# Two kept products ahead of the fourth chunk, and an imaginary weight of mode 0 that is not read, in a fused attention and spectral-mixing kernel

## The chip, the cores and the metric

The kernel runs on one core of a Trainium2 chip. The metric is device time in microseconds of one execution. A core has a matrix engine (PE, with PEld for its weight loads), a vector engine (DVE), a scalar engine (ACT), GpSimd (POOL), which here issues the loads, SyncE (SP), which here issues the small copies and the stores, and 16 DMA engines that all transfers share.

## The reference

Attention with a learned decay runs first; its output is the input of a spectral layer: a Fourier transform along the sequence (576 positions), the 64 lowest modes each multiplied by a complex 512x512 matrix, the inverse transform, and a last matrix with a ReLU.

```python
def _moe_ref(x, w_r, w_i, w_ch):          # x: 8 x 576 x 512, the attention's output
    X = np.fft.rfft(x, axis=1)
    Xr, Xi = (np.real(X[:, :n_modes]), np.imag(X[:, :n_modes]))
    Yr = np.einsum('bmd,mde->bme', Xr, w_r) - np.einsum('bmd,mde->bme', Xi, w_i)
    Yi = np.einsum('bmd,mde->bme', Xr, w_i) + np.einsum('bmd,mde->bme', Xi, w_r)
    Y[:, :n_modes] = Yr + 1j * Yi
    y = np.fft.irfft(Y, n=S, axis=1)
    u = x + y
    return u + np.maximum(u @ w_ch, 0.0)
```

For mode 0 the imaginary part Xi is a sum of x times sin(0), so it is zero, and the inverse transform multiplies Yi of mode 0 by sin(0). The matrix `w_i` of mode 0 therefore has no part in the output.

## The kernel before

**Attention and transform.** The 512 channels are cut into NG = 4 groups of 128 (two heads each), and the attention runs over N = 32 steps n, one for each group and batch. A step makes scores, exponentials and the products with v, then `fft` writes the group's 64 modes into `xs`. The loads of q, k, v for the steps ahead and of the weights `w_r`, `w_i` are issued by POOL in one order (`load`, L220); they are read as fp32 and written as bf16.

**The weights.** A tile holds 4 modes of one group and one of the two weights (ri = 0 real, 1 imaginary): `wq` (L182) lists them as (g, c, ri, par), where c is one of 8 chunks of 8 modes and par its half. There are 128 tiles, 32 for each group. A tile is loaded by two transfers (L210 to L216): even modes into partitions 0 to 63, odd ones into 64 to 127, two modes and 256 KB of bf16 each. The first 8 tiles lie in memory that is free at the start; later ones in rings of buffers, for the last group in one ring of 11 (`wpool`). A tile's load waits until the products of the tile 11 places before it are done.

**The modes.** `modes(g, c)` (L442) makes 16 products of 512 columns that fill one PSUM bank `yp`, four side by side in the columns of the array (128 rows by 32 columns each); x = 0, 1 are those with the real weight, x = 2, 3 with the imaginary one. The results of the groups are added in `y_acc`. In the last group the sum is `y_sb`, in fp16.

**The last group.** After the attention (L573) POOL issues all loads that are left. Per chunk c, L773 to L795 go: `modes`, then `y_transposed` (4 transpositions of `y_sb`, one copy by ACT), and from c = 4 on `y_times_wch` (4 products with `w_ch`). After c = 3 `gather` brings the first four chunks into the order that the inverse transform needs (`yv`); after c = 5 it does so for chunks 4 and 5.

**Kept products.** The output comes in 18 pairs of 128-row blocks. x times `w_ch` doesn't depend on the weights of the modes, so for 16 pairs it is made early and kept in SBUF. 10 of them (`late`, L701) are made in the last group: a call of `work` (L689) transposes the x of one pair (`x_transposed`, L604) and makes the product of the pair before it (`keep`, L625; ACT copies it, and for half of the pairs DVE subtracts). `TAKE` (L703) says how many calls each chunk has; `gather` after c = 3 has two more (turns 1 and 3). `places` (L592 to L595) are 9 places for kept products, the tenth takes a ring buffer. Pairs 0 and 1 are not kept: their products (`x_times_wch`, L616) stay in PSUM for the end.

**The end.** The modes of c = 7 are made with other work in between: `first_u` ahead of x = 2, `first_z` ahead of x = 3 (L798 to L808). Then PE makes the inverse transforms of all pairs, ACT and DVE finish them, and SP stores them.

Of the kernel before, what the change touches and what calls it, by code (L numbers as in the profile page):

```python
# [18 lines left out]
def kernel(  # L19
# [15 lines left out]
    P = 128  # L35
# [10 lines left out]
    MC = 8  # L46
    NCK = NM // MC
# [10 lines left out]
    HP = P // 2  # L58
# [87 lines left out]
    def loads_qkv(n):  # L146

        if n >= N:
            return []
        g, b = divmod(n, B)  # L150
        hs = slice(2 * g, 2 * g + 2)
        q2 = qkpool.tile([P, R + 1, D], BF16, name="q2", tag="q2")[:, :R, :]
        k2 = qkpool.tile([P, R + 1, D], BF16, name="k2", tag="k2")[:, :R, :]
        loaded[n] = (q2, k2)
        todo = [
            (dst, src[b, hs].rearrange("h (p r) d -> (h p) r d", r=R))
            for src, dst in ((q, q2), (k, k2))
        ]
        todo += [
            (  # L160
                v2[n % NV][:, : 2 * NWN * W].rearrange("p (w h c) -> p w h c", w=NWN, h=2)[:, :, h, P:],
                v[b, 2 * g + h, : NF * P, :].rearrange("(w p r) d -> p w (r d)", p=P, r=2),
            )
            for h in range(2)
        ]
        return todo

    def loads_tails(g):

        if g >= NG:  # L170
            return []
        return [
            (
                v4[g % 2][NL * h : NL * h + NL, :, :D],
                v[:, 2 * g + h, NF * P :, :].rearrange("b t d -> t b d"),
            )
            for h in range(2)
        ]
# [11 lines left out]
    wt = {}  # L190
# [3 lines left out]
    def ring_of(k):  # L194
        if k < NE:
            return None
        return int(k < LW2 and (k - NE) % (WA + WB) >= WA)

    def loads_w(upto):
        todo = []  # L200
        while len(wt) < min(upto, len(wq)):
            g, c, ri, par = key = wq[len(wt)]
            i = ring_of(len(wt))
            if i is None:
                t = early[len(wt)]
            else:
                t = (wpool, wpool2)[i].tile([P, WM, DM], BF16, name="w_sb", tag="w")
            src = (moe_w_r, moe_w_i)[ri]
            m0 = c * MC + par * MC // 2
            for h in range(2):  # L210
                todo.append((
                    t[HP * h : HP * h + HP].rearrange("p (m q) e -> p m (q e)", q=2),
                    src[m0 + h : m0 + MC // 2 : 2, g * P : (g + 1) * P, :].rearrange(
                        "m (p q) e -> p m (q e)", q=2
                    ),
                ))  # L216
            wt[key] = t
        return todo
# [34 lines left out]
    first, second, tails0 = loads_qkv(0), loads_qkv(1), loads_tails(0)  # L253
    load(first[:2])
    load(loads_w(W0), first[2:] + tails0 + second)
    nc.sync.dma_start(out=Ff_sb, in_=d_Ff.rearrange("(T p) c -> p T c", p=P))
    nc.sync.dma_start(out=ident16h, in_=d_ident16h)
# [184 lines left out]
    def modes(g, c, meanwhile=None):  # L442


        ps = auxpool.tile([P, DM], FP32, name="yp", tag="aux")
        cols = xs[g % 2].rearrange("p q k h r b m -> p q k (h r b) m")

        def product(ri, q_, cg):
            nc.tensor.matmul(  # L449
                ps[32 * cg : 32 * cg + 32, :],  # L450
                cols[:, q_, 1 - ri, :, c * MC // 2 + cg],
                wt[(g, c, ri, cg // 2)][:, 2 * (cg % 2) + q_, :],
                start=(ri == 0 and q_ == 0), stop=(ri == 1 and q_ == 1),
                tile_position=(0, 32 * cg), skip_group_check=True,
            )

        for x in range(4):
            ri, y = divmod(x, 2)
            if meanwhile and x in meanwhile:
                meanwhile[x]()  # L460
            for z in range(4):
                if meanwhile:
                    product(ri, z // 2, 2 * y + z % 2)
                else:
                    product(ri, y, z)
        if g == 0:
            nc.vector.tensor_copy(out=y_acc[:, c, :], in_=ps)
        elif g < NG - 1:
            nc.vector.tensor_tensor(out=y_acc[:, c, :], in0=ps, in1=y_acc[:, c, :], op=ALU.add)
        else:  # L470
            yb = spool.tile([P, DM], FP16, name="y_sb", tag="y")
            for cols in halves if c == NCK - 1 else [slice(0, DM)]:
                nc.vector.tensor_tensor(
                    out=yb[:, cols], in0=ps[:, cols], in1=y_acc[:, c, cols], op=ALU.add
                )
            if c >= NCK - 2:
                spread(c, 0, yb)
            return yb
# [3 lines left out]
    def spread(c, which, rows):  # L482

        nc.sync.dma_start(out=yv[16 * c : 16 * c + 16, :, which, :], in_=rows)
# [97 lines left out]
    upool = ctx.enter_context(tc.tile_pool(name="u_psum", bufs=2, space=PSUM))  # L582
    zpool = ctx.enter_context(tc.tile_pool(name="z_psum", bufs=2, space=PSUM))

    NLOC = 4
    old = xs_flat[0]
    xt_sb = [
        old[:, i * 2 * DM : (i + 1) * 2 * DM].bitcast(FP16).rearrange("p (x t c) -> p x t c", x=2, c=P)
# [3 lines left out]
    places = [finpool.tile([P, 4 * DM], BF16, name="r_sb", tag="r", bufs=3) for i in range(2)]  # L592
    places += [finpool.tile([P, 4 * DM], BF16, name=f"z1_{i}") for i in range(NLOC)]
    places.append(old[:, 4 * DM : 8 * DM])
# [3 lines left out]
    def parts(b, T):  # L598

        if T < NF:  # L600
            return [(slice(0, P), b, ident16h)]
        return [(slice(NL * i, NL * i + NL), b + i, ident16h[:NL, :NL]) for i in range(2)]

    def x_transposed(i):  # L604
        xts[i] = xt_sb[len(xts) % 2]
        for x, (b, T) in enumerate(pairs[i]):
            ps = upool.tile([P, DT, P], FP32, name="xt_ps", tag="u")
            for rows, bb, ident in parts(b, T):
                for dt in range(DT):
                    nc.tensor.matmul(  # L610
                        ps[:, dt, rows], x_all[: rows.stop - rows.start, dt, bb, T, :],
                        ident, start=True, stop=True, skip_group_check=True,
                    )
            nc.vector.tensor_copy(out=xts[i][:, x], in_=ps)

    def x_times_wch(i, last):  # L616
        zs[i] = z = zpool.tile([P, 2, DM], FP32, name="z_ps", tag="z")
        for x in range(2):
            for dt in range(DT):
                nc.tensor.matmul(  # L620
                    z[:, x, :], xts[i][:, x, dt, :], wch_sb[:, dt, :],
                    start=(dt == 0), stop=(last and dt == DT - 1), skip_group_check=True,
                )
# [13 lines left out]
    NY = NCK // 2  # L637
    yt_first = finpool.tile([P, DT, NY, P], FP16, name="yt_first")

    def y_transposed(yb, c=NCK):  # L640
        ps = auxpool.tile([P, DT, P], FP16, name="yt_ps", tag="aux")
        for dt in range(DT):
            nc.tensor.transpose(ps[:, dt, :], yb[:, bass.ts(dt, P)], ident16h)
        yt = yt_first[:, :, c % NY, :] if c < NCK - 2 else spool.tile([P, DT, P], FP16, name="yt_sb", tag="yt")
        nc.scalar.copy(out=yt, in_=ps)
        return yt

    def y_times_wch(c, yt):
        vp = auxpool.tile([P, DM], FP32, name="v_ps", tag="aux")
        for dt in range(DT):  # L650
            nc.tensor.matmul(
                vp, yt[:, dt, :], wch_sb[:, dt, :], start=(dt == 0), stop=(dt == DT - 1)
            )
        vb = spool.tile([P, DM], FP16, name="v_sb", tag="v")
        nc.vector.tensor_copy(out=vb, in_=vp)
        spread(c, 1, vb)
        return vb
# [31 lines left out]
    def work():  # L689

        if not order_z and not ahead:
            return
        if order_z:
            i = order_z.pop(0)
            x_transposed(i)
            ahead.append(i)
        if len(ahead) == 2 or not order_z:
            i = ahead.pop(0)
            keep(i)

    late = [i for i in kept if i not in first_pairs]  # L701
    order_z = list(late)
    TAKE = (3, 2, 2, 0, 1, 1)  # L703
    us, rs = {}, {}
    GK = P - 2 * MC * NX

# [66 lines left out]
    for c in range(NCK - 2):  # L773
        yb = modes(NG - 1, c)
        for x in range(TAKE[c] - 1):
            work()
        if c == NCK - 3:
            x_transposed(0)
        yt = y_transposed(yb, c)
        if TAKE[c]:  # L780
            work()
        if c >= NY:
            y_times_wch(c, yt)
            if c == NCK - 3:
                gather(NY, NCK - 2, (), (0,))
        elif c == NY - 1:
            gather(0, NY, (1, 3), (1, 0))
    assert not order_z and not ahead
    c = NCK - 2
    x_times_wch(0, False)  # L790
    yb6 = modes(NG - 1, c)
    x_transposed(1)
    yt = y_transposed(yb6)
    x_times_wch(1, False)
    vb6 = y_times_wch(c, yt)  # L795


# [104 lines left out]
```

## Time and profile before

| | |
|---|---|
| median of 11 runs | 454.19 us (452.46 to 455.35) |
| the profiled execution | 453.26 us, its span 451.5 us |
| PE busy | 356.1 us (79%) |
| DVE, ACT, POOL busy | 257.4, 222.0, 241.1 us |
| moved by DMA | 93.83 MB, mean 208 GB/s |
| weight transfers by POOL | 120 + 120 in `w_sb`, 256 KB each, 8.0 and 8.1 us to landing; 16 more into other tiles |
| products of `modes` (L449) | 480 in the records, 444 ns each |

Times of the profile run from the first instruction of the span. Each digit of a row of slices is the busy share of one fortieth of the span. In a row of the timeline come start and duration in us, the engine, the line, the operation, the tiles, how many were merged, and in brackets the engine's idle time before it with what ended it.

### The profile page before, as it was taken

The page shows a single profiled execution, that of the slowest core. Times are in us where ns is not written, and L with a number is a line of the kernel's source. Part 1 is how long each engine was busy: PE and PEld are TensorE (multiplying, and loading weights), DVE is VectorE, ACT ScalarE, POOL GpSimd, SP SyncE. Part 2 cuts the span into 40 slices and gives each one's busy share as a digit, 9 for nine tenths or more (in the row PEclk, how much of TensorE's full clock was granted, in tenths as well). Part 3 has the DMA queues.
Part 4 walks back from the last instruction along what each step waited for, and adds up shares of the span by engine and source line. Part 5 has one row for each costly group of instructions (what it writes and reads, how often), then busy time and mean ns, then how long its engine had stood idle before and what let it go on. Part 6 is the DMA issues. An engine that isn't in the chain of part 4 may idle for free.

```text
span 451.5 us, 11547 instructions
## 1 busy us (share of the span) xinstructions
PE 356.1 (79%) x4713; PEld 225.4 (50%) x4745; DVE 257.4 (57%) x599; ACT 222.0 (49%) x390; POOL 241.1 (53%) x397
## 2 busy tenths in 40 slices
PE   1789988998574979856978687778897778879995
PEld 1466666565443656633546454556564335534432
DVE  7675767574333646733436545546656443662796
ACT  1585778366232745743426443556551223331774
POOL 7766665755566666555665765565544444420000
PEclk9996999897567969987659968989999986999999
DMA  9999999999999999999999999999999999994688
GB/s 180 201 204 206 204 204 205 205 206 207 208 207 202 200 186 200 208 208 206 204 203 207 207 206 207 207 205 201 205 210 211 209 209 209 210 219 91 234 300 316
DMA packets 77797, 93.83 MB, mean 208 GB/s; under 512 B 30433, under 2 KB 40161, under 8 KB 77745
## 3 DMA queue, kind: packets, MB, share of 16 engines
q0 software_dynamic: 68240, 81.81, 104.8%
q1 hardware_dynamic: 9504, 11.29, 7.9%
q8 instruction: 37, 0.61, 0.5%
q14 instruction: 16, 0.12, 0.1%
HBM read 164.56 MB, written 9.44 MB: 385 GB/s over the span
## 4 chain that ended last, share of the span: by engine, by line
DMA 48%; PE 33%; DVE 10%; issue 4%; POOL 2%; ACT 1%; DVEq 0%; POOLq 0%; ACTq 0%
DMA w_sb<-in_moe_w_i_dram 26%; DMA w_sb<-in_moe_w_r_dram 7%; DMA q<-in_q_dram 7%; PE av_ps L401 4%; PE yp L449 4%; PE sc_ps L372 4%; PE ft_ps L427 3%; DMA k<-in_k_dram 3%; PE sc_ps L366 3%; PE tr_ps L331 2%; DVE qtB L334 2%; PE z_ps L620 2%; PE z_ps L711 2%; DVE qtA L334 2%; PE g_ps L670 2%
## 5 line engine op out<-in xcount | busy, mean ns | idle before, releaser
L380 ACT ACTIVATE p_sb<-sc_ps,cumt_sb 128x576 f16<-128x576 f32 (+1 forms) x256 | 141.8, 635 | 59.0 <-PE sc_ps L372 58.6
L224 POOL DMA_DIRECT2D w_sb<-in_moe_w_r_dram x120 | 71.6, 597 | 60.3 <-DMA w_sb<-in_moe_w_r_dram 18.5
L224 POOL DMA_DIRECT2D w_sb<-in_moe_w_i_dram x120 | 71.5, 596 | 49.3 <-DMA w_sb<-in_moe_w_i_dram 15.8
L224 POOL DMA_DIRECT2D v<-in_v_dram x72 | 51.8, 719 | 25.3 <-DMA w_sb<-in_moe_w_i_dram 7.6
L366 PE MATMUL sc_ps<-negm,ident 128*128 128x256 bf16 x256 | 56.8, 309 | 0.2
L449 PE MATMUL yp<-w_sb,xs 128*32 128x512 bf16 x480 | 39.9, 444 | 10.0 <-DMA w_sb<-in_moe_w_i_dram 5.6
L401 PE MATMUL av_ps<-v,p_sb 128*128 128x65 f16 x1024 | 46.1, 201 | 0.0
L334 DVE COPY ktA<-tr_ps 64x576 bf16<-64x576 bf16 x32 | 24.0, 749 | 36.1 <-PE tr_ps L331 36.1
L331 PE MATMUL tr_ps<-ident,q 64*64 64x64 bf16 x576 | 17.2, 209 | 34.1 <-DMA q<-in_q_dram 34.0
L401 PEld LDWEIGHTS <-p_sb 128*128 128x128 f16 x1024 | 40.2, 102 | 5.3 <-DVE x_all L411 2.0
L334 DVE COPY qtA<-tr_ps 64x576 bf16<-64x576 bf16 x32 | 23.8, 743 | 30.7 <-PE tr_ps L331 30.6
L372 PE MATMUL sc_ps<-qtA,ktA 65*128 65x512 bf16 (+2 forms) x192 | 38.3, 311 | 0.6 <-DMA qtA<-ncum_sb 0.6
L351 ACT ACTIVATE p<-sc_ps,cumt 128x64 f16<-128x64 f32 x32 | 10.0, 313 | 55.5 <-PE sc_ps L347 55.5
L437 DVE CAST xs<-ft_ps 64x128 bf16<-64x128 f32 x128 | 31.4, 284 | 9.1 <-PE ft_ps L427 8.7
L372 PE MATMUL sc_ps<-qtB,ktB 128*128 128x64 bf16 (+2 forms) x160 | 33.7, 314 | 3.3 <-issue 2.0
L406 DVE TENSOR_REDUCE den<-av_ps 128x5 f32<-128x10 f32 x64 | 10.8, 169 | 44.3 <-PE av_ps L401 43.5
L427 PE MATMUL ft_ps<-Ff_sb,x_all 128*64 128x96 f16 (+1 forms) x640 | 34.0, 228 | 1.0 <-DVE x_all L411 1.0
L331 PE MATMUL tr_ps<-ident,k 64*64 64x64 bf16 x576 | 16.7, 205 | 20.4 <-DVE qtB L334 10.8
L411 DVE TENSOR_TENSOR x_all<-av_ps,rcp 128x320 f16<-128x320 f32 x64 | 31.5, 492 | 2.2
L334 ACT COPY ktB<-tr_ps 64x576 bf16<-64x576 bf16 x32 | 20.3, 633 | 24.5 <-DVE ktA L334 23.4
L331 PEld LDWEIGHTS <-q 64*64 64x64 bf16 x576 | 13.4, 121 | 36.7 <-DMA q<-in_q_dram 35.5
L449 PEld LDWEIGHTS <-xs 128*32 128x32 bf16 x512 | 19.3, 147 | 24.1 <-issue 13.5
(117 smaller groups left out, 555.7 us busy)
## 6 DMA issues: line engine op xcount, KB each, us to landing
w_sb<-in_moe_w_r_dram POOLq DMA_DIRECT2D x120, 256.0 KB, 8.0
w_sb<-in_moe_w_i_dram POOLq DMA_DIRECT2D x120, 256.0 KB, 8.1
q<-in_q_dram POOLq DMA_DIRECT2D x32, 144.0 KB, 7.3
k<-in_k_dram POOLq DMA_DIRECT2D x32, 144.0 KB, 7.2
v<-in_v_dram POOLq DMA_DIRECT2D x72, 64.0 KB, 7.0
out_dram<-r_sb SPq DMA_DIRECT2D x16, 256.0 KB, 2.2
out_dram<-r_w SPq DMA_DIRECT2D x16, 256.0 KB, 2.7
x_all<-in_moe_w_i_dram POOLq DMA_DIRECT2D x6, 256.0 KB, 7.2
```

The costliest lines, as they stand in the source:

```text
L224: nc.gpsimd.dma_start(out=dst, in_=src)
L331: nc.tensor.transpose(ps[rows, r, :], src[rows, r, :], ident16[rows, rows])
L334: copy(out=dst[n % NQ][rows, :].rearrange("d (p r) -> d p r", r=R), in_=ps[rows].rearrange("d r p -> d p r"),)
L366: nc.tensor.matmul(ps[:, bass.ds(w * S, W)], ident16, negm[:, bass.ts(r, W)], start=True, stop=False, skip_group_check=True,)
L372: nc.tensor.matmul(ps[:, c0 : c0 + i1 - i0], keys[:, w, r, :], qt[:, i0:i1], start=False, stop=True, skip_group_check=True,)
L380: nc.scalar.activation(out=pt[:, poff[x] : poff[x] + S - w * W], in_=ps[:, w * S : (w + 1) * S - w * W], func=ACTF.Exp, bias=cumt_sb[:, x, ...
L401: nc.tensor.matmul(ps[:, I, r : r + NCH], lhsT, rhs, start=(i == 0), stop=(i == len(todo) - 1), skip_group_check=True,)
L406: nc.vector.tensor_reduce(out=den, in_=ps[:, :, 0 : VW : NCH], axis=mybir.AxisListType.X, op=ALU.add)
L411: nc.vector.tensor_tensor(out=x_all[:, g, b, :, D * h : D * h + D], in0=ps[:, :, 1 : NCH], in1=rcp.unsqueeze(2).to_broadcast([P, NT, D]), ...
L427: nc.tensor.matmul(ps[HP * h : HP * h + HP, q_, :], x_all[:nT, g, b, T, q_::2], Ff_sb[:nT, T, 3 * HM * h : 3 * HM * (h + 1)], start=(T == ...
L437: nc.vector.tensor_copy(out=xs[g % 2][rows, :, k, h, :, b, :], in_=ps[rows, :, k * HM : (k + 2) * HM].rearrange("p q (r m) -> p q r m", r=2),)
L449: nc.tensor.matmul(ps[32 * cg : 32 * cg + 32, :], cols[:, q_, 1 - ri, :, c * MC // 2 + cg], wt[(g, c, ri, cg // 2)][:, 2 * (cg % 2) + q_, ...
```

## The change

It has two parts. The load of tile (g, 0, 1, 0), which holds the imaginary weights of modes 0 to 3, leaves out mode 0: the transfer into partitions 0 to 63 brings one mode and not two. The two products of each group that would use mode 0 take rows 64 to 127 alone (mode 1). So this part leaves out a factor that is always zero or meets a zero.

In the last group, c = 2 has four calls of `work` and not two, and c = 4 and c = 5 have none; c = 3 keeps its two in `gather`. A fifth place `z1_4` holds a kept product, so none takes a ring buffer. Pairs 0 and 1 are transposed and multiplied in chunks 4 and 5, and no longer around c = 6.

```diff
             for h in range(2):
+                first = 1 if ri == 1 and m0 + h == 0 else 0
                 todo.append((
-                    t[HP * h : HP * h + HP].rearrange("p (m q) e -> p m (q e)", q=2),
-                    src[m0 + h : m0 + MC // 2 : 2, g * P : (g + 1) * P, :].rearrange(
+                    t[HP * h : HP * h + HP, 2 * first :].rearrange("p (m q) e -> p m (q e)", q=2),
+                    src[m0 + h + 2 * first : m0 + MC // 2 : 2, g * P : (g + 1) * P, :].rearrange(
...
         def product(ri, q_, cg):
+            k0 = HP if ri == 1 and c == 0 and cg == 0 else 0
             nc.tensor.matmul(
                 ps[32 * cg : 32 * cg + 32, :],
-                cols[:, q_, 1 - ri, :, c * MC // 2 + cg],
-                wt[(g, c, ri, cg // 2)][:, 2 * (cg % 2) + q_, :],
+                cols[k0:, q_, 1 - ri, :, c * MC // 2 + cg],
+                wt[(g, c, ri, cg // 2)][k0:, 2 * (cg % 2) + q_, :],
                 start=(ri == 0 and q_ == 0), stop=(ri == 1 and q_ == 1),
-                tile_position=(0, 32 * cg), skip_group_check=True,
+                tile_position=(k0, 32 * cg), skip_group_check=True,
             )
...
-    NLOC = 4
+    NLOC = 5
...
-    TAKE = (3, 2, 2, 0, 1, 1)
+    TAKE = (3, 2, 4, 0, 0, 0)
...
         yb = modes(NG - 1, c)
         for x in range(TAKE[c] - 1):
             work()
-        if c == NCK - 3:
-            x_transposed(0)
+        if c >= NY:
+            x_transposed(c - NY)
         yt = y_transposed(yb, c)
         if TAKE[c]:
             work()
         if c >= NY:
+            x_times_wch(c - NY, False)
             y_times_wch(c, yt)
...
     c = NCK - 2
-    x_times_wch(0, False)
     yb6 = modes(NG - 1, c)
-    x_transposed(1)
     yt = y_transposed(yb6)
-    x_times_wch(1, False)
     vb6 = y_times_wch(c, yt)
```

## The prediction, made before the changed kernel was run

> **What bounds the kernel now.** I read four views. First the page's slices and its chain of waits, over the whole run:
>
> ```profile
> DMA  9999999999999999999999999999999999994688
> GB/s 180 201 204 206 204 204 205 205 206 207 208 207 202 200 186 200 208 208 206 204 203 207 207 206 207 207 205 201 205 210 211 209 209 209 210 219 91 234 300 316
> DMA 48%; PE 33%; DVE 10%; issue 4%; POOL 2%; ACT 1%; DVEq 0%; POOLq 0%; ACTq 0%
> ```
>
> The transfer engines are full in every slice until about 406 us, at 200 to 210 GB/s with one dip to 186. Where the chain passes through PE for a while (27 to 104, 162 to 193, 228 to 244 us), the engines stay fed: a weight transfer lands a median 8.0 us after its issue, so about six are under way whatever PE does. Up to 370 us, then, this is a transfer-bound kernel.
>
> Second, the timeline of PE and POOL around the last group's fourth chunk (c=3), where the chain changes over:
>
> ```profile
> 366.55 1.08 PE L449 MATMUL yp<-w_sb,xs 128*32 128x512 bf16 x10
> 370.21 1.07 PE L449 MATMUL yp<-w_sb,xs 128*32 128x512 bf16 x6 [2.58 <-DMA w_sb<-in_moe_w_i_dram]
> 373.35 1.99 PE L670 MATMUL g_ps<-wch_sb,yt_first 128*64 128x512 f16 x8 [0.67 <-ACT yt_first L645]
> ...
> 381.88 1.14 PE L670 MATMUL g_ps<-wch_sb,yt_first 128*64 128x512 f16 x8
> ...
> 390.33 0.61 PE L610 MATMUL xt_ps<-ident16h,x_all 128*128 128x128 f16 x8
> 390.78 1.89 PE L620 MATMUL z_ps<-wch_sb,xs 128*128 128x512 f16 x8
> ...
> 412.85 0.65 PE L449 MATMUL yp<-w_sb,xs 128*32 128x512 bf16 x4
> ```
>
> PE stands 2.58 us for c=3's last weight, and never again for a weight: from 370.21 to the end the chain is work on PE, with short DVE and ACT steps. Third, the same stretches with the granted clock (the third number from the end of a row, ahead of the DMA share and the GB/s):
>
> ```profile
> 366.60:370.20 3.60, 1.03 (x11) 0.44 (x11) 1.13 (x2) 1.01 (x1) 1.61 (x3) 0.97 1.12 210
> 370.20:380.20 10.00, 7.57 (x51) 4.98 (x51) 2.83 (x5) 2.70 (x5) 4.74 (x9) 0.50 1.12 209
> 380.20:388.20 8.00, 7.01 (x60) 4.62 (x58) 5.01 (x9) 3.13 (x5) 4.01 (x7) 1.00 1.12 209
> 418.00:446.00 28.00, 27.01 (x131) 10.92 (x130) 24.00 (x39) 21.26 (x22) 0.00 (x0) 1.00 0.81 285
> ```
>
> After the wait PE runs at half clock for 10 us: the same eight gather products take 1.99 us there and 1.14 us later. And from 418 to 446 PE is busy 27 of 28 us at full clock: what comes after the last chunk moves as one block. Fourth, the last weight transfer and its landing:
>
> ```profile
> 400.29 0.59 POOL L224 DMA_DIRECT2D w_sb<-in_moe_w_i_dram  x1 [0.46 <-DMA w_sb<-in_moe_w_i_dram]
> DMA to landing us min/median/max: 11.8/11.8/11.8
> ```
>
> It lands at 400.3 + 11.8 = 412.1 us, and its four products (x=3 in `modes`) start at 412.85. **So PE leads and the stream is only 0.75 us behind it**: this small margin decides what a faster PE is worth.
>
> **The weight that is not read.** In each of four groups one of two transfers of tile (g, 0, 1, 0) is halved: 64 rows of one mode in place of two, 128 KB of the 256 KB of bf16 written. POOL issues four weight transfers each 5.0 us (381.69, 386.71, 391.72, 396.73), 1.25 us each, so a half is 0.63 us and four are 2.5 us. They were issued at 10.6, 119.4, 230.6 and 326.3 us, all while the engines are full, so every later landing comes earlier by what was saved. Bounds: 2.5 above; below 1.2, if two of the four fall where PE paces POOL (230.6 us lies in the chain's PE stretch 228 to 244). The Trainium skill, "DMA: Bandwidth & Descriptors", section "Anatomy of one DMA — SWDGE (gpsimd) path", prices a transfer at about 2.0 us plus bytes over 436 GB/s, which would make an estimated 0.3 us of each half and 1.2 us of four. That fits a transfer on its own; the row, a full queue at 210 GB/s, is the nearer, and I take 2.5 (S below).
>
> The 8 products with 64 instead of 128 rows stay 8, as long as before (512 columns each). The trace shows no 64x32 tile. A rule speaks against it: "TensorEngine Tiling (Array Packing)", section "Tiling Modes", says that a change of tiling mode drains TensorE. Here the 128*32 products at 349.36 (1.10 us) are followed by 128*128 ones at 350.39 with no gap. By the row it costs 0; by the rule, each odd product alone and not four abreast is at most 0.38 us (the shortest L449 product) each way, 1.5 us a chunk. I take 0: in the last group chunk 0 is followed by 3 us of waiting for weights (0.90 and 2.11 us before 359.72), and in the others the queue of six transfers hides it.
>
> **The products that move.** A call of `work` is one transposition (8 products, 0.61) and one kept product (8, 1.89): 2.2 us at 390.33 to 392.50, up to 2.6 with small waits; two are 4.9. They now stand ahead of c=3.
> - Before: c=2 ends at 360.79 (it waits for its own last weight), two calls and `y_transposed` take 5.82, c=3 starts at 366.55, waits, ends at 371.28.
> - After: c=2 ends at 360.8 - S; 5.82 + 4.9 later c=3 starts at 371.5 - S. Its last weight lands at 370.2 - S, so the wait is gone, and c=3 ends at 372.6 - S: 1.3 us later than a pure shift.
> - The gather behind it no longer runs cold. Its first half took 373.35 to 381.88 (8.5 us), its second, warm, 6.3; the second call in it has no transposition left (0.62). It takes 12.0 for 14.8 us, starting about 1.9 after c=3's end: c=4 starts at 386.5 - S, before 388.18. Here a rule and the row part: "TensorE: Matmul & The Clock Gate", Part 1, asks for an idle window of about 3.4 us before the clock halves; the row shows 2.58 us of idling enough. By the rule the gain ends with the wait; by the row there are 2.2 us more, which I take.
> - c=4 and c=5 now do `x_transposed` and `x_times_wch` of pairs 0 and 1 where they did kept work: the same products, less c=4's kept subtract (1.22 us on DVE), which delayed c=5's `y_sb` to 395.49. About 0.6.
> - The product of pair 0 ahead of c=6 goes (1.90 at 400.40), but gains nothing: c=6 waited for the copies of `yv` on DVE until 402.35, and does still. Behind c=6, pair 1's goes (405.73): ACT's copy of `yt_sb` (0.58 to 406.15) comes late instead, so 1.3.
> - c=7 starts at about 404.9 - S, before 408.42: **3.5 us more than S on PE.**
>
> **What is late next.** The stream does not gain from this. With PE at 404.9 - S, chunk 7's second tile lands at 406.3 - S (395.2 + 11.1), its third at 408.7 - S (397.75 + 10.9), its fourth at 412.1 - S. PE waits 1.0, about 0.6 and 1.0 us, with `first_u` and `first_z` between, and x=3 starts at 412.1 - S: 0.75 us is left of 3.5. The spread of `v_sb` on SP's queue, 409.25 before, now runs ahead of the last weights and not beside their end; this may cost 0.3 or free up to 0.9 us.
>
> No load is held up: chunk 6's last tile takes the buffer of chunk 4's first (eleven buffers), issued at 389.21 - S, and released at about 387 - S. The fifth `z1` place saves the last kept product a ring buffer; result buffers come one slot earlier, from chunks long done. SP's order and the number of products stay.
>
> **Sum:** 2.5 + 0.75 = 3.25 us. The profiled execution took 453.26 us (span 451.5), 0.9 under the median of 454.19: 450.0 against its own time, 450.9 against the median.
>
> **Rivals.**
> 1. The stream's end is not binding (0.13): the last landing took 11.8 us where 8 is usual, because spreads shared the engines. If these lie apart, most of PE's 3.5 counts: 2.5 + 2.9 = 5.4 us, 448.8. Against: the engines were full in both cases.
> 2. The saved read does not arrive (0.12): PE's stretches swallow it, and only the 0.75 is left: 453.4. For: the chain runs through PE at 228 to 244. Against: no slice there falls below 203 GB/s.
> 3. Slower (0.15): the waits within chunk 7 (2.6 us in sum, the size that halved the clock at 370) let the clock fall just ahead of the dense tail. 10.2 us at half clock, as then, cost 5.1 us of PE: 454.2 - 3.25 + 5.1 = 456.0. It decides from 6.5 us of half clock on. Against: these waits are broken up by work, and the like pattern at 403 to 406 (1.13 and 0.20 idle) kept the clock at 1.00.
>
> **Numbers.** The forecast has 0.60, by itself 450.0 to 452.5 (S from 1.2, spreads 0.9 better). With rivals 1 and 2 the range is 448.8 to 453.4. About 0.2% (0.9 us) is what can be told from no change: faster 0.73, within it 0.12, slower 0.15.
>
> **What would show it.** Right: no wait at c=3, clock 1.00 through the gather, a new wait for `w_sb` in chunk 7 of 0.5 to 1.5 us before its last products, the last weight landing near 409.6, and a tail of the same length. Wrong: the last landing not 2 us earlier (the read), c=4 starting later than 385 us (the reorder), a 0.5 clock behind chunk 7 (rival 3).

## The result, and the profile after

| | before | after |
|---|---|---|
| median | 454.02 us (47 runs) | 450.74 us (12 runs, 449.89 to 452.12) |
| ratio to before, 95% interval | | 0.993 (0.9916 to 0.9943) |
| profiled execution, its span | 453.26, 451.5 us | 450.67, 448.9 us |
| last weight packet ends | 411.23 us | 408.90 us |
| first of the last four products of the modes | 412.85 us | 410.30 us |
| from there to the end of the span | 38.6 us | 38.6 us |

3.3 us less by the medians, where 3.25 was forecast (450.9). The two profiled executions differ by 2.6 us, and all of that lies ahead of the last products of the modes: the tail behind them kept its length. First the page of the changed kernel, slices and chain:

```profile
DMA  9999999999999999999999999999999999994688
GB/s 176 199 204 206 204 203 205 203 206 206 207 207 202 202 187 200 208 206 207 205 202 206 208 205 206 208 204 203 209 210 211 209 210 210 209 217 90 237 300 315
```

```profile
DMA 44%; PE 36%; DVE 9%; issue 4%; POOL 3%; ACT 3%; DVEq 0%; ACTq 0%; POOLq 0%
```

The transfer engines are as full as before, at the same rate; less is moved (93.31 MB, not 93.83). PE's share of the chain grows from 33% to 36%: from 340.86 us to the end the chain now holds no wait for a transfer, where before it left the transfers at 370.21. Next the timeline of PE in the last group (start, duration, engine, line):

```profile
340.86 2.44 PE L451 MATMUL yp<-w_sb,xs 128*32 128x512 bf16 x16 [1.09 <-DVE xs L438]
...
351.93 1.09 PE L451 MATMUL yp<-w_sb,xs 128*32 128x512 bf16 x16
...
358.19 1.09 PE L451 MATMUL yp<-w_sb,xs 128*32 128x512 bf16 x16
...
369.55 1.09 PE L451 MATMUL yp<-w_sb,xs 128*32 128x512 bf16 x16
...
372.54 1.14 PE L672 MATMUL g_ps<-wch_sb,yt_first 128*64 128x512 f16 x8 [0.68 <-ACT yt_first L647]
...
382.00 1.14 PE L672 MATMUL g_ps<-wch_sb,yt_first 128*64 128x512 f16 x8 [1.60 <-DVE yv L682]
...
398.91 1.09 PE L451 MATMUL yp<-w_sb,xs 128*32 128x512 bf16 x16 [1.87 <-DVE yv L682]
401.69 0.60 PE L645 MATMUL yt_ps<-ident16h,y_sb 128*128 128x128 f16 x4 [1.69 <-DVE y_sb L475]
402.97 1.89 PE L653 MATMUL v_ps<-wch_sb,yt_sb 128*128 128x512 f16 x4 [0.68 <-ACT yt_sb L647]
404.79 1.08 PE L451 MATMUL yp<-w_sb,xs 128*32 128x512 bf16 x8
405.81 1.03 PE L732 MATMUL u_ps<-x_all,ident16h 128*128 128x512 f16 x2
...
410.30 0.65 PE L451 MATMUL yp<-w_sb,xs 128*32 128x512 bf16 x4
```

The fourth chunk (369.55) has no bracket: its wait of 2.58 us is gone, and so is the third chunk's (358.19). The gather's first products take 1.14 us, not 1.99. New are three gaps around the seventh chunk (1.87, 1.69, 0.68 us), and behind them slow work: the four products at 402.97 took 1.89 us, before the change 1.03. The granted clock tells why (third number from the end of a row):

```profile
370.20:380.20 10.00, 7.51 (x80) 5.52 (x69) 4.78 (x8) 4.36 (x8) 4.72 (x8) 1.00 1.12 210
...
397.00:400.40 3.40, 1.12 (x19) 0.51 (x16) 2.08 (x4) 1.73 (x3) 1.18 (x2) 1.00 1.11 208
400.40:403.80 3.40, 1.44 (x7) 0.62 (x7) 1.20 (x2) 0.59 (x1) 0.00 (x0) 0.50 1.13 223
```

Around the gather the clock is now whole. It falls later, at 400.4 us, for 6.8 us, right behind 3.4 us in which PE was busy for 1.12. So the last products of the modes had no wait for a weight in this execution: PE itself was the late one. The last two weight transfers, by issue and landing:

```profile
L225 POOL DMA_DIRECT2D w_sb<-in_moe_w_i_dram x2: 590/590/590, 398.1 to 398.8; - x2
...
DMA to landing us min/median/max: 9.9/10.2/10.5
```

They were in place by 398.8 + 10.5 = 409.3 us at the latest, 1 us ahead of the products at 410.30.

### The profile page after: what moved, and what is told of

It reads as the page before. It is cut to its first block, busy times and chain, and to the rows that moved or that the text cites. A ratio compares the mean times of both kernels' runs of the same rounds, so it can differ in the third digit from the quotient of the medians.

```text
span 448.9 us, 11548 instructions
## 1 busy us (share of the span) xinstructions
PE 361.2 (80%) x4713; PEld 227.8 (51%) x4745; DVE 257.4 (57%) x599; ACT 222.5 (50%) x390; POOL 240.9 (54%) x397
## 2 busy tenths in 40 slices
DMA packets 77540, 93.31 MB, mean 208 GB/s; under 512 B 30432, under 2 KB 40160, under 8 KB 77488
## 4 chain that ended last, share of the span: by engine, by line
DMA 44%; PE 36%; DVE 9%; issue 4%; POOL 3%; ACT 3%; DVEq 0%; ACTq 0%; POOLq 0%
DMA w_sb<-in_moe_w_r_dram 17%; DMA w_sb<-in_moe_w_i_dram 10%; DMA k<-in_k_dram 7%; DMA q<-in_q_dram 5%; PE z_ps L622 5%; PE yp L451 5%; PE av_ps L402 4%; PE ft_ps L428 3%; PE sc_ps L373 3%; PE sc_ps L367 2%; PE tr_ps L332 2%; PE z_ps L713 2%; PE u_ps L732 2%; DMA y_acc<-in_moe_w_r_dram 2%; PE u_ps L713 2%
## 5 line engine op out<-in xcount | busy, mean ns | idle before, releaser
L402 PE MATMUL av_ps<-v,p_sb 128*128 128x65 f16 x1024 | 47.4, 203 | 0.0
L451 PE MATMUL yp<-w_sb,xs 128*32 128x512 bf16 (+1 forms) x480 | 39.8, 422 | 7.2 <-DVE yv L682 1.9
L402 PEld LDWEIGHTS <-p_sb 128*128 128x128 f16 x1024 | 41.7, 104 | 5.4 <-DVE x_all L412 1.8
L373 PE MATMUL sc_ps<-qtA,ktA 65*128 65x512 bf16 (+2 forms) x192 | 40.8, 326 | 0.6 <-DMA qtA<-ncum_sb 0.6
L451 PEld LDWEIGHTS <-xs 128*32 128x32 bf16 (+1 forms) x512 | 19.3, 145 | 21.8 <-issue 11.3
```

Of the source, the lines that this page charges most:

```text
L373: nc.tensor.matmul(ps[:, c0 : c0 + i1 - i0], keys[:, w, r, :], qt[:, i0:i1], start=False, stop=True, skip_group_check=True,)
L402: nc.tensor.matmul(ps[:, I, r : r + NCH], lhsT, rhs, start=(i == 0), stop=(i == len(todo) - 1), skip_group_check=True,)
L451: nc.tensor.matmul(ps[32 * cg : 32 * cg + 32, :], cols[k0:, q_, 1 - ri, :, c * MC // 2 + cg], wt[(g, c, ri, cg // 2)][k0:, 2 * (cg % 2) + ...
```

## The experiments

Twelve kernels, each against runs of the kernel before on the same chip. Ratios have their 95% intervals; 0.0022 is 1 us.

### The two halves of the change

`read_only` is the kernel before with the first half of the diff alone.

> The kernel before with the unread weight alone (its 64-row products too), the order of the products as before. Theory of the stream: every landing comes 2.3 us earlier (the last weight packet ended 2.34 us earlier in the changed kernel), PE still stands for the fourth chunk's weight and then runs at half clock, and the time falls by 2.3 us to about 451.7 (ratio 0.995). Rival: the 64-row products, which in the changed kernel made the last group's first chunk 2.44 us instead of 1.09, and PE's stretches swallow it: less than 1 us, above 453.

`order_only` is the changed kernel with that half undone:

```diff
-                first = 1 if ri == 1 and m0 + h == 0 else 0
-                    t[HP * h : HP * h + HP, 2 * first :]...
+                    t[HP * h : HP * h + HP]...
...
-            k0 = HP if ri == 1 and c == 0 and cg == 0 else 0
```

> The changed kernel with the whole weight read and the products over 128 rows as before; only the order is changed. Theory: the fourth chunk's wait and the half clock behind it go, but the last weight lands where it did before (412.1 us), so the last four products of the modes start 0.5 to 0.8 us earlier than before (412.85) and the time falls by 0.5 to 1.0 us, to 453.0 to 453.5. Rival: the order is worth all of the 3 us that PE saves ahead of the last chunk: 451. Second rival: without filler around the seventh chunk the clock falls as in the changed kernel (400.4 to 407.2 us), and what is gained is at most 0.3.

Measured: the read alone 451.56 us, 0.9952 (0.9938 to 0.9967), 2.2 us less (1.5 to 2.8). The order alone 453.95 us, 1.0015 (0.9999 to 1.0031): no gain. In the profile of `read_only`, PE's fourth chunk:

```profile
365.50 0.43 PE L451 MATMUL yp<-w_sb,xs 128*32 128x512 bf16 x2 [1.62 <-DMA w_sb<-in_moe_w_i_dram]
367.98 0.65 PE L451 MATMUL yp<-w_sb,xs 128*32 128x512 bf16 x6 [2.05 <-DMA w_sb<-in_moe_w_i_dram]
...
370.71 1.98 PE L672 MATMUL g_ps<-wch_sb,yt_first 128*64 128x512 f16 x8 [0.68 <-ACT yt_first L647]
```

As before the change PE stands for the weights, then gathers at half clock (1.98), only earlier: 367.98 for 370.21. That is the stream's theory. In the profile of `order_only`, the end of the modes:

```profile
400.12 1.93 PE L449 MATMUL yp<-w_sb,xs 128*32 128x512 bf16 x16 [1.88 <-DVE yv L680]
402.90 0.61 PE L643 MATMUL yt_ps<-ident16h,y_sb 128*128 128x128 f16 x4 [0.85 <-DVE y_sb L473]
...
406.01 1.09 PE L449 MATMUL yp<-w_sb,xs 128*32 128x512 bf16 x8
...
412.14 0.65 PE L449 MATMUL yp<-w_sb,xs 128*32 128x512 bf16 x4
```

PE begins the last chunk 2.4 us earlier than before (406.01 for 408.42), but cold; the last products start 0.7 us earlier (412.14 for 412.85), and the last weight packet ended where it did (411.34 for 411.23). The size is that of the forecast's 0.75 us, the way is not: no bracket names a weight here, so PE at half clock (399.6 to 409.8 us), and not the last landing, set this start. The median doesn't show the gain, and the profiled execution, 452.51 us, was the fastest of the 14.

### Does the clock take back what the order gives?

`filler6` moves pair 1's product into the gap ahead of the seventh chunk; `order_filler6` is the same without the read.

```diff
         if c >= NY:
-            x_times_wch(c - NY, False)
+            if c == NY:
+                x_times_wch(0, False)
             y_times_wch(c, yt)
...
+    x_times_wch(1, False)
     yb6 = modes(NG - 1, c)
```

> The changed kernel with pair 1's product moved from the sixth chunk to just ahead of the seventh chunk's products, where PE stood 1.87 us. If the half clock from 400.4 to 407.2 us is what made the last chunk late, the clock stays at 1.00 there, PE reaches the last chunk about 2 us earlier and then waits for its weights; the last weight landed 0.5 us before it was used, so the time falls by about 0.5 us only, to 450.2. If the new waits let the clock fall in the tail: slower than the changed kernel by 2 us or more, 453. If the gap was harmless: 450.7.

> The new order alone (the whole weight is read), with pair 1's product ahead of the seventh chunk. The new order alone came to the time before, with half clock from 399.6 to 409.8 us. If this half clock took back what the order gave, the time is now 0.7 to 1.0 us under that of before (ratio 0.998), bounded by the last weight's landing, which the order doesn't move. If the order is worth nothing for another reason: ratio 1.000.

Measured: `filler6` 450.32 us, 0.9923 (0.991 to 0.9936), 0.3 us under the changed kernel and not told apart from it. `order_filler6` 453.24 us, 0.9988 (0.9977 to 1.0000), where the order alone had 1.0015: about 1.2 us better, the intervals just touching. In its profile the clock still fell, but for 3.4 us (404.2 to 407.6) where the order alone had 10.2. In the profile of `filler6`:

```profile
402.90 0.65 PE L451 MATMUL yp<-w_sb,xs 128*32 128x512 bf16 x4
404.31 0.65 PE L451 MATMUL yp<-w_sb,xs 128*32 128x512 bf16 x4 [0.76 <-DMA w_sb<-in_moe_w_r_dram]
...
407.97 0.65 PE L451 MATMUL yp<-w_sb,xs 128*32 128x512 bf16 x4 [1.61 <-DMA w_sb<-in_moe_w_i_dram]
...
410.39 0.65 PE L451 MATMUL yp<-w_sb,xs 128*32 128x512 bf16 x4
```

```profile
400.40:403.80 3.40, 2.01 (x12) 0.73 (x12) 1.10 (x2) 0.58 (x1) 0.00 (x0) 1.00 1.13 217
403.80:407.20 3.40, 2.06 (x10) 0.70 (x10) 0.00 (x0) 0.00 (x0) 0.00 (x0) 1.00 1.11 217
407.20:410.60 3.40, 2.63 (x14) 1.09 (x16) 0.00 (x0) 0.00 (x0) 0.00 (x0) 1.00 0.43 74
```

With the gap filled the clock stays whole, and now PE does what the forecast had it do: it comes 1.9 us earlier to the last chunk (402.90 for 404.79) and waits for weights in it. Not all of the 1.9 us is the clock: pair 1's product no longer stands ahead of the gather's copies, so the seventh chunk itself starts 0.8 us earlier (398.08 for 398.91). From there to the last chunk it is 4.82 us, where the changed kernel took 5.88 (398.91 to 404.79): 1.06 us is what the half clock cost up to there.

The last products start where they did (410.39). They come 2.42 us behind those of 407.97, as they did before the change (410.43 to 412.85): that is PE's work in between, so what bounds this execution is the third tile's weight more than the last one's. Its stream was also later: the last weight packet ended at 410.06 us, for 408.90 in the changed kernel, with the same bytes read. The waits, 2.4 us in sum, let no clock fall.

`take_read` keeps, of the new order, only the two kept products (`TAKE` and `NLOC` on top of `read_only`).

> The unread weight and, of the new order, the two kept products ahead of the fourth chunk alone; pairs 0 and 1 stay around the seventh chunk as in the kernel before. If the gap that they left there is what cost the clock: clock 1.00 around the seventh chunk, the last products bounded by the weights, and a time as with the moved filler, 450.3. If the order in chunks 4 and 5 mattered by itself: 451 or more, as with the read alone (451.6).

Measured: 450.38 us, 0.9928 (0.9906 to 0.9949): the time as expected, the way not. PE came to the seventh chunk 3.7 us earlier than in the changed kernel and stood there:

```profile
399.36 1.07 PE L451 MATMUL yp<-w_sb,xs 128*32 128x512 bf16 x6 [3.12 <-DMA w_sb<-in_moe_w_i_dram]
...
401.82 3.60 PE L622 MATMUL z_ps<-wch_sb,xs 128*128 128x512 f16 x8
```

3.12 us of waiting, then half clock (398.7 to 405.5 us; eight products in 3.60 us, not 1.89) and the last products at 410.74. So the time doesn't tell pairs 0 and 1 in their old place from the new one. That the two kept products are worth something is not shown either: the intervals of `take_read` and `read_only` (0.9938 to 0.9967) overlap.

### What bounds the last chunk, stream or PE?

`end_free_after` leaves the last chunk's two imaginary tiles of the last group unread (the products take the real ones, so the output's last modes are others): 1 MB off the stream's end. `end_free` does so to `filler6`.

```diff
             g, c, ri, par = key = wq[len(wt)]
+            if key[:3] == (3, 7, 1):
+                wt[key] = wt[(3, 7, 0, par)]
+                continue
```

> The changed kernel, with the same two tiles not read. In its profile PE ran at half clock from 400.4 to 407.2 us and came to its last products without a wait. If that is what bounds it, taking 1 MB off the end of the stream changes nothing, or up to 0.4 us: 450.3 to 450.7. If the stream's end bounds it as forecast: 449 or less.

> The moved filler (pair 1's product ahead of the seventh chunk), and the two imaginary tiles of the last chunk of the last group are not read: their products use the real tiles instead, so 1 MB less of bf16, all of it at the end of the stream. If the stream's end bounds the moved filler's kernel (PE stood 0.76 and 1.61 us for weights in the last chunk), the second wait goes and the time falls by 1.2 to 2 us, to about 448.7. If PE bounds it: no change, 450.3.

`warm_end` adds 17 unread products to `end_free_after`, `warm_filler6` 9 to `filler6`:

```diff
+    warm(8)        # not in warm_filler6
     yb6 = modes(NG - 1, c)
+    warm(7)
     yt = y_transposed(yb6)
+    warm(2)
```

> The changed kernel without the two tiles at the stream's end, as before, and with 17 products more whose result nobody reads, in the three gaps around the seventh chunk (8 ahead of its products, 7 behind them, 2 behind its transpositions). They add work and move none. If the half clock (397.7 to 407.9 us without them) is what holds the last chunk there, the clock stays at 1.00, the last products of the modes start 1.5 to 2 us earlier and the time falls from 450.3 to about 448.6. If the gaps were harmless: the same or slower, 450.3 to 451.

> The kernel with the moved filler and with 9 unread products in the two gaps left around the seventh chunk. Its clock was at 1.00 there in the profile already, and PE waited 0.76 and 1.61 us for weights in the last chunk: bounded by the stream's end, so no change, 450.0 to 450.6, only with less spread. If its clock falls in most runs that weren't profiled: 0.5 us faster or more.

| | median | ratio | last products (profile) |
|---|---|---|---|
| `end_free_after` | 450.26 | 0.9921 (0.9906 to 0.9935) | 410.09 |
| `end_free` | 449.58 | 0.9915 (0.9896 to 0.9933) | 408.02 |
| `warm_end` | 449.72 | 0.9911 (0.9891 to 0.9931) | 409.19 |
| `warm_filler6` | 450.15 | 0.9926 (0.9904 to 0.9948) | 409.79 |

`end_free_after` met its expectation: with the stream out of the way the changed kernel gains 0.4 us by the ratios, not told apart from none. `warm_filler6` didn't change, as expected. `end_free` and `warm_end` came in the expected direction in the profile, but by their ratios they lie only about 0.4 us under their partners (`filler6` and `end_free_after`), where 1.2 to 2 was expected. `end_free`'s executions ran from 448.44 to 451.0, and the profiled one was the fastest. In it the second wait is gone (no bracket at 405.60):

```profile
403.62 0.65 PE L454 MATMUL yp<-w_sb,xs 128*32 128x512 bf16 x4 [0.70 <-DMA w_sb<-in_moe_w_r_dram]
...
405.60 0.65 PE L454 MATMUL yp<-w_sb,xs 128*32 128x512 bf16 x4
...
408.02 0.65 PE L454 MATMUL yp<-w_sb,xs 128*32 128x512 bf16 x4
```

`warm_end` is the cleanest test of the gaps, since it only adds work. Here are the starts of the seventh and the last chunk, first in `end_free_after`, then in `warm_end`:

```profile
397.77 1.93 PE L454 MATMUL yp<-w_sb,xs 128*32 128x512 bf16 x16 [1.87 <-DVE yv L685]
...
403.65 1.26 PE L454 MATMUL yp<-w_sb,xs 128*32 128x512 bf16 x8
```

```profile
399.02 1.09 PE L454 MATMUL yp<-w_sb,xs 128*32 128x512 bf16 x16
...
403.84 0.65 PE L454 MATMUL yp<-w_sb,xs 128*32 128x512 bf16 x4
```

From one chunk to the other it took 5.88 us at half clock, and 4.82 with nine products more in between, at a clock of 1.00. That the gaps let the clock fall, and what it costs PE, is shown by this pair of profiles; that it reaches the medians is not.

So stream and cold PE bound the end within a microsecond of each other, and the executions of one kernel differ by more than that. Which of the two decides in a given execution of the changed kernel is shown for the profiled one only.

### Does a saving in PE's stretch arrive?

`group2` reads what the changed kernel leaves out, and leaves out one tile in its place, on top of `order_only` (its output lacks that weight):

```diff
+            if key == (2, 0, 1, 0):
+                wt[key] = wt[(2, 0, 0, 0)]
+                continue
```

> The changed order with 512 KB less to read in one place: in place of a half tile in each of four groups, the whole tile (2, 0, 1, 0) is not read (its products use the real tile), so nothing of the 64-row products either. Its two transfers were issued at 230.6 and 231.8 us, in a stretch where the chain of waits runs through PE. If what is saved there arrives at the end (full queue): the time of the changed kernel, 450.7 (ratio 0.993). If PE's stretch swallows it: that of the new order alone, 453.5 (ratio 1.000).

Measured: 451.15 us, 0.9947 (0.9929 to 0.9966), against 1.0015 of the order alone, intervals far apart: about 3 us for 512 KB, saved at 230 us where the chain ran through PE. It arrives.

### The odd tile shape

`zero_fill` has GpSimd write zeros into the unread rows and multiplies 128 rows again (`k0 = 0`); `odd_last` puts the two 64-row products together at their chunk's end.

```diff
+                if first:
+                    todo.append((t[:HP, :2], None))
...
+            if src is None:
+                nc.gpsimd.memset(dst, 0.0)
```

```diff
+            if c == 0 and x >= 2:   # 128-row products first, then product(1, 0, 0), product(1, 1, 0)
```

> The changed kernel with the unread 64 rows filled with zeros by GpSimd and the products of mode 0 over 128 rows again: the same read, no odd tile shape. Theory: the first chunk of the last group takes 1.1 us again, not 2.44, and the clock doesn't halve at 342 us; but then PE waits for weights behind it, so the time is that of the changed kernel within 0.5 us (450.2 to 450.9). Rival: the odd shape costs 1 us or more on the path in each group: 449 or less.

> The changed kernel with the two 64-row products of a group put one after the other at the end of their chunk, and not each ahead of three 128-row ones. Theory: a product of another tile shape runs alone and lets the others wait, so two changes of shape fewer shorten the last group's first chunk from 1.8 us between its first and last start to 1.2 to 1.5; behind it PE has slack, so the time is that of the changed kernel, 450.2 to 451. If the shape were on the path: 449.7 or less.

The weight loads of the last group's first chunk in the changed kernel, whose 16 products took 2.44 us:

```profile
341.45 0.13 PEld L451 LDWEIGHTS <-xs 64*32 64x32 bf16 x1 [0.37 <-issue]
341.81 0.14 PEld L451 LDWEIGHTS <-xs 128*32 128x32 bf16 x3 [0.23 <-issue]
342.18 0.13 PEld L451 LDWEIGHTS <-xs 64*32 64x32 bf16 x1 [0.23 <-issue]
342.66 0.14 PEld L451 LDWEIGHTS <-xs 128*32 128x32 bf16 x3 [0.35 <-issue]
```

and the same chunk's products in `zero_fill`:

```profile
342.86 1.09 PE L456 MATMUL yp<-w_sb,xs 128*32 128x512 bf16 x16 [1.09 <-DVE xs L443]
```

From a 64-row product to the next start it is 0.36 us (341.45 to 341.81), and as long for the three behind it, where four 128-row ones side by side take about 0.21 (16 in 1.09 us, 8 in 0.66). Part of the 2.44 us is half clock (342.4 to 349.2 us), and that comes without the shape too: `order_only` has no 64-row product, and its clock was halved from 341.6 to 348.4 us:

```profile
340.82 1.31 PE L449 MATMUL yp<-w_sb,xs 128*32 128x512 bf16 x16 [1.10 <-DVE xs L437]
...
350.93 1.10 PE L449 MATMUL yp<-w_sb,xs 128*32 128x512 bf16 x16
...
359.84 0.65 PE L449 MATMUL yp<-w_sb,xs 128*32 128x512 bf16 x6 [1.77 <-DMA w_sb<-in_moe_w_i_dram]
```

From the first chunk to the second it is 11.07 us in the changed kernel (340.86 to 351.93), 10.11 here, and 7.90 in `zero_fill` and in the kernel before, both of which kept the clock: 2.2 us for the half clock and 1.0 for the shape. The second group shows the shape's 1.0 us at full clock:

```profile
169.29 1.96 PE L449 MATMUL yp<-w_sb,xs 128*32 128x512 bf16 x32 [0.18 <-DVE xs L437]
```

```profile
167.55 2.98 PE L451 MATMUL yp<-w_sb,xs 128*32 128x512 bf16 x32 [0.36 <-DVE xs L438]
```

(the kernel before, then the changed one.) `zero_fill` took 451.63 us, 0.9948 (0.9928 to 0.9969), and `odd_last` 450.60 us, 0.9942 (0.9928 to 0.9957). `odd_last` shortened its chunk little: 1.7 us between the first and last start, where 1.8 was to become 1.2 to 1.5, with half clock from 338.8 us on (2.25 us for the chunk). Neither is told apart from the changed kernel, so no time is shown for the shape; that it is off the path isn't shown either, since the changed kernel's chain runs through this chunk. `zero_fill` came to 7.90 us, then stood 1.76 us for the third chunk's weight (as expected), and its last weight packet ended at 410.87, 2.0 us later than in the changed kernel. Why its stream ended so late is open; each of its fills holds GpSimd, which issues the loads, for 0.97 us.

## Why the prediction was right

**The saved read (2.5 us) held.** Alone it measured 2.2 us (1.5 to 2.8), and the last packet of the changed kernel ended 2.33 us earlier (in the profile of `read_only` 1.6). The row it was sized by, 1.25 us for a transfer in a full queue, came nearer than the estimate from the Trainium skill's price ("DMA: Bandwidth & Descriptors", section "Anatomy of one DMA — SWDGE (gpsimd) path"), 1.2 us for the four. Rival 2, a saving lost in PE's stretches, fell with `group2`.

**The wait and the cold gather went as forecast,** and the clock followed the row, not the rule of the Trainium skill ("TensorE: Matmul & The Clock Gate", Part 1) that it halves after an idle window of about 3.4 us: PE was busy for 1.12 of the 3.4 us ahead of the half clock at 400.4. The gather took 12.8 us where 12.0 was forecast, since a kept product's subtraction (1.23 us on DVE) now lies between its copies: 1.60 us of waiting at 382.00 where 0.99 was usual.

**The products of 64 rows were not free,** as had been taken from the row: they cost PE 1.0 us a chunk. That fits the Trainium skill ("TensorEngine Tiling (Array Packing)", section "Tiling Modes"), by which a change of tiling mode drains TensorE; the forecast's bound from it was 1.5. The half clock behind the first chunk, another 2.2 us, was not foreseen. PE came to the third chunk 2.6 us later than before (358.19 for 355.62) and its last weight 2 us earlier (issued at 347.56, landed 10.0 us later, about 1 us ahead of its products), so the wait that was to stay there went too. So the cover named in the forecast (PE waits for weights behind the chunk) didn't hold in the profiled execution: from the first chunk on PE's lateness was carried to the end.

**The step that failed is PE's arrival at the last chunk.** 404.9 - 2.5 = 402.4 us was forecast, 404.79 measured. Of these 2.4 us, 1.3 were there at the fifth chunk (385.31 for 384.0): 0.5 from the later start of the fourth and 0.8 from the gather. By the forecast's own sign (a fifth chunk later than 385 us) the term of the reorder was wrong. The rest, 1.1 us, is the half clock around the seventh chunk, behind the gap that the moved product left: the forecast saw the gap gain nothing and did not see that it would cost. The forecast chain of waits in chunk 7 therefore didn't occur in the changed kernel; it occurred in `filler6` (0.76 and 1.61 us) when the gap was filled. The half clock took another 1.1 us within the last chunk (5.51 us from its first to its last products, 4.43 before). The forecast had let most of PE's 3.5 us go unused in waits for the stream, so all this lateness moved the last products only from the forecast 409.6 to 410.30.

**The order's 0.75 us is the weakest term.** On top of the read it is worth 1.0 us (0.993 for 0.9952, intervals overlapping slightly), alone nothing (1.0015), with the gap filled 0.5 us alone. None of these pairs settles it. That the sum came out at 3.28 us for 3.25 is in part luck: the last products came 2.55 us earlier in the profiled pair, 2.33 of it the stream's, and the wait that was to yield the 0.75 wasn't there.

**Rivals.** Rival 1 (the stream's end doesn't bind, so PE's whole lead counts, 448.8) fell as a time. Its premise was true of the profiled execution, where no weight was waited for; but the lead was gone by then. Where the clock stayed whole (`filler6`), PE stood for the weights. Rival 3 named the right mechanism in the wrong place: the clock fell ahead of the last chunk, from gaps between DVE and ACT steps, and for 6.8 us, which ended short of the dense tail. Waits within chunk 7 (`filler6`) left it whole.

None of the variants is told apart from the changed kernel as faster; `filler6` has the lowest median of those that compute the whole output but one (`warm_filler6`, 450.15), within their intervals.

## What to carry to other kernels

In a stretch bound by a full transfer queue, bytes not read were worth about their share of the queue's rate, also where PE was on the chain when they were saved. Work moved out of a place leaves a gap there: ask what the gap does to the clock and not only whether the engine had slack. And before counting a faster engine's lead, look how far the stream's last landing is behind it: that margin is all that it can win.

## What was not expected of the hardware

Clock steps came at distances of 3.4 us or multiples. Cutting the traces along these steps, PE busy for 0.43, 1.13, 1.12 and 0.95 of 3.4 us was followed by half clock; 1.80, 2.01, 2.06 and 2.07 were not. These rows of the kernel before stand for the two sides:

```profile
366.50:369.90 3.40, 1.13 (x11) 0.48 (x11) 1.23 (x3) 1.01 (x1) 1.71 (x3) 1.00 1.11 208
404.00:407.40 3.40, 2.07 (x12) 1.03 (x13) 2.24 (x4) 0.58 (x1) 0.00 (x0) 1.00 1.12 222
```

But the busy share draws no sharp line. Around the last group's first chunk the clock fell behind 1.76 busy us of 3.4 in `order_only` and 1.92 in `group2`, both without a 64-row product. And it fell behind 2.31 in the changed kernel, where `zero_fill` kept it behind the same busy time in the same stretch of work (both stretches end 1.54 us behind the chunk's start). The rows of `order_only`, the changed kernel and `zero_fill`:

```profile
338.20:341.60 3.40, 1.76 (x36) 1.19 (x36) 1.96 (x6) 0.00 (x0) 1.54 (x3) 1.00 1.13 211
```

```profile
339.00:342.40 3.40, 2.31 (x33) 1.07 (x27) 1.47 (x5) 0.00 (x0) 1.77 (x3) 0.99 1.11 208
```

```profile
341.00:344.40 3.40, 2.31 (x44) 1.43 (x38) 1.83 (x6) 0.00 (x0) 1.32 (x3) 1.00 1.12 211
```

The last two differ in the 64-row products, so it may matter what PE is busy with. That is one pair of executions, and nothing here tests it.
